# A new written order for the opening of a state-attention and feed-forward kernel, and a last tile scaled by one engine

## The chip, the cores and the metric

The kernel runs on one core of one Trainium2 chip. The metric is the time of one execution on the device in microseconds (us); the median of three runs is given. One of them, or one like them, was also taken with the hardware profiler, which records what each engine does and when. The engines are TensorE (PE in the rows, its weight loads PEld), VectorE (DVE), ScalarE (ACT), GpSimd (POOL) and SyncE (SP, which here only issues transfers).

## What is computed

Eight batches of eight heads attend between 512 tokens and 32 state rows of width 64, in both directions. The joined result (4352 rows of 512) goes through a feed-forward layer with a clipped activation.

```python
def _attn_ref(x, state):                      # x (8, 8, 512, 64), state (8, 8, 32, 64)
    scores = scale * np.matmul(x, state.transpose(0, 1, 3, 2))
    scores = scores - scores.max(-1, keepdims=True)
    a = np.exp(scores)
    a /= a.sum(-1, keepdims=True) + 1e-09
    xread = np.matmul(a, state)
    ...                                       # the same from state to tokens: sread
    return np.concatenate([xread, sread], axis=2)

def _moe_ref(x, w_in, w_out):                 # w_in (512, 2048), w_out (2048, 512)
    h = x @ w_in
    relu6 = np.clip(h + 3.0, 0.0, 6.0)
    g = h * relu6 / 6.0
    return g @ w_out
```

## The kernel before

**The work.** `xread @ w_in` is computed as the attention weights times `W = state @ w_in`, so a batch needs its weights `aT` and its `W` (tiles `wp`). A step n is one slice of 128 of the 2048 hidden columns of one batch: `first(n)` makes `ps_h` from `wp` and `aT`, ScalarE and VectorE make the activation `g`, and `second(n)`, two steps later, adds `g` times a slice of `w_out` into four accumulators `acc0` to `acc3`. A product in float32 is made of two halves of 32-bit operands (`hi`, `lo`) with three matmuls; `split` makes the halves with one pass on ScalarE and one on VectorE. The very first step and its `wp` stay whole float32 (L1011, L1059). There are 8 batches of 16 steps, and at the end 16 more steps for the state rows of all batches.

**The opening.** Before the first product of `first(0)` (L1011) batch 0 needs its attention weights. Its tokens come in four quarters of two heads each (tile `xb`, L496). Quarters 1 and 3 are issued by ScalarE's queue, behind the state (L452). Quarters 0 and 2 are issued by SyncE's queue, and the first slice of `w_in` (tile `early`, L387) stands between them. For each quarter q, TensorE turns the tokens into bank `acc{q}` (four transposes, L641), ScalarE copies them to `w_in3` (L645), and TensorE makes the scores (L708). The state is turned by one transpose (L610), and VectorE spreads it over `sread_t` with four copies (L619); the scores need these. Then the softmax of a quarter runs: VectorE takes the maximum (L719) and subtracts it (L727), ScalarE takes the exponential (L730), VectorE sums (L733). For two quarters at a time VectorE makes the reciprocal (L738), and the multiplication (L741) is GpSimd's for quarters 0 and 1 and VectorE's for quarters 2 and 3. TensorE turns the result (L750), the copies go to `w_in2` (L752, L753), and `first(0)` begins.

**The weights.** They come as loads of 64-bit words of which ScalarE writes the upper part (`tops`, L396) and VectorE joins both (L401). `W` for the first slices (L529) needs the joined `w_in0`.

**What sets the order.** Every operation is told to a `Plan` with an engine, a cost and a rank. The plan walks through them with its own clock and puts them in a row; each engine then runs its own in that order, and waits where data is missing. For the first operations the row isn't planned but written out: `OPENING` is a list of operation numbers. In it 0, 2, 3 and 4 are the loads of quarters 0, 1, 2 and 3, 1 is the state's load, 24 the first `w_in` load, 27 the state's transpose, 34, 36, 38 and 40 the transposes of the quarters, 42, 47, 54 and 59 their scores. Where the plan's clock sees TensorE idle before `first(0)`, `issue` puts small matmuls on constants there (L1442). 27 of them run.

**The end.** The last tile of the output is `acc1` times 1/6. It is cut in two: ScalarE scales columns 0 to 255, VectorE the others (L1087), and one transfer stores it.

Of the kernel before, what the change touches and what calls it, by code (L numbers as in the profile page):

```python
# [45 lines left out]


OPENING = """
# [25 lines left out]
"""  # L74


class Plan:
# [3 lines left out]


    AFTER = {"T": 0.25, "V": 0.12, "S": 0.12, "P": 0.15, "Q": 0.0}
    WARM = 5.9

    first_loads = 5

# [131 lines left out]
def tile_state_attention_then_hardswish_ffn(  # L219
# [8 lines left out]
    nc = tc.nc  # L228
    B, H, S, D = x.shape
    NS = state.shape[2]  # L230
    DFF = w_in.shape[1]
    DO = w_out.shape[1]
# [8 lines left out]
    NF = DFF // P  # L241
# [51 lines left out]
    def T(cost, rank, do, reads=(), writes=(), after=()):  # L293
        return plan.add("T", cost, rank, do, reads, writes, after)

    def V(cost, rank, do, reads=(), writes=(), after=()):
        return plan.add("V", cost * 1.08 if states_told else cost, rank, do, reads, writes, after)
# [307 lines left out]
    def take_in(b, rank, after=(), banks=None):  # L605

        st = ("ps_s", ("st", b))
        rank = rank if isinstance(rank, list) else [rank] * 3
        if b < TURNED:
            T(0.12, rank[0], lambda: nc.tensor.transpose(  # L610
                bank(st)[:, :P], made["st_raw", b], ident),
                [("st_raw", b)], [st], after)

        for r in range(2) if b < TURNED else ():
            for i in range(2):
                def put(r=r, i=i):
                    src = bank(st)[r * D : (r + 1) * D, :P].rearrange("p (q u m) -> p q u m", q=NQ, u=NG)
                    dst = apart[i * D : (i + 1) * D, :, :, i].rearrange("p q u (m r) -> p q u m r", r=2)
                    nc.vector.tensor_copy(dst[..., r], src)  # L619
                V(0.22, RANKS["apart"] if b == 0 else URGENT, put, [st], [("apart", b, r, i)])  # L620
        for u in range(NG) if b < TURNED else ():
            def together(u=u):
                rows = slice(u * D, (u + 1) * D)
                stT = get(("stT", b), lambda: att.tile([P, P], F32, name="stT"))
                nc.gpsimd.tensor_copy(
                    stT[rows].rearrange("p (q n) -> p q n", n=NS), apart[rows, :, u, u])
            kept.append(P_(0.3, RANKS["apart"], together, apart_parts(b), [("stT", b)]))
        for q in range(NQ):
            if b >= TURNED:
                key = ("raw", ("x", b, q // 2))  # L630
                V(0.7, rank[0], lambda q=q, key=key: nc.vector.transpose(  # L631
                    xT(b, q), made[key][:, q % 2]),
                    [(*key, q % 2, u, k) for u in range(2) for k in range(D // NS)], [xT_key(b, q)], after)
                continue
            ps = (banks[q] if banks else "ps_s", ("T", b, q))

            def turn(q=q, ps=ps):
                for u in range(NG):
                    for k in range(J // 2):
                        twos = x_tile(b)[:, NG * q + u, 2 * k : 2 * k + 2, :]  # L640
                        nc.tensor.transpose(  # L641
                            bank(ps)[:, (u * 2 + k) * P : (u * 2 + k + 1) * P],
                            twos.rearrange("p j d -> p (j d)"), ident)
            T(0.45, rank[1], turn, [(*x_key(b), "q", q)], [ps], after)
            S_(0.6, rank[2], lambda q=q, ps=ps: nc.scalar.copy(xT(b, q), bank(ps)), [ps], [xT_key(b, q)], [table])  # L645
# [42 lines left out]
    def tokens_by_rows(after, banks):  # L688
# [11 lines left out]
        for q in range(NQ):  # L700
# [3 lines left out]
            def scores(q=q, ps=ps):  # L704
                out = bank(ps)[:, : A * NS].rearrange("p (k i u n) -> p k u i n", k=J // 2, i=2, n=NS)
                for u in range(NG):
                    for k in range(J // 2):
# [6 lines left out]
            m1 = lambda m1_key=m1_key: get(  # L714
                m1_key, lambda: small.tile([P, S // NS], F32, name="m1"))[:, :A]
            r = RANKS["soft0"]
            scores_at[0] = T(0.93, RANKS["scores0"], scores,
                             apart_parts(0) + [xT_key(0, q)], [ps], after)
            V(0.34, r[0], lambda m1=m1, view=view: nc.vector.tensor_reduce(  # L719
                m1(), view(), axis=AX.X, op=ALU.max), [ps], [m1_key])  # L720
# [328 lines left out]
    def second(n):  # L1049
# [26 lines left out]
        for j in range(nt):  # L1076
            acc = (f"acc{j}", seg)
            rank = n + LAG
            if more:
                V(0.68, rank, lambda j=j, acc=acc: nc.vector.scalar_tensor_tensor(  # L1080
                    ot()[:, j, :], bank(acc), 1.0 / 6.0, ot()[:, j, :], op0=ALU.mult, op1=ALU.add),
                    [acc], [(*ot_key, j)])
            elif b == B and j == nt - 1:
                for add, engine, cs in (
                    (S_, nc.scalar.mul, slice(0, DO // 2)), (V, nc.vector.tensor_scalar_mul, slice(DO // 2, DO))
                ):
                    add(0.42, rank, lambda j=j, acc=acc, engine=engine, cs=cs: engine(  # L1087
                        ot()[:, j, cs], bank(acc)[:, cs], 1.0 / 6.0), [acc], [(*ot_key, j, cs.start)])
            elif b < B and (j % 2 == 0 or i < NF - 1):
                S_(0.62, rank, lambda j=j, acc=acc: nc.scalar.mul(ot()[:, j, :], bank(acc), 1.0 / 6.0),  # L1090
                   [acc], [(*ot_key, j)])
            else:
                V(0.68, rank, lambda j=j, acc=acc: nc.vector.tensor_scalar_mul(
                    ot()[:, j, :], bank(acc), 1.0 / 6.0), [acc], [(*ot_key, j)])
# [8 lines left out]
        else:  # L1103

            ov = out.rearrange("(b s) e -> s b e", s=TOK)
            for j in range(nt):
                rows = slice(S + j * P // B, S + (j + 1) * P // B)
                parts = [(*ot_key, j)] if j < nt - 1 else [(*ot_key, j, k * DO // 2) for k in range(2)]
                Q(n, 262.0, lambda j=j, rows=rows: nc.sync.dma_start(ov[rows], ot()[:, j, :]), parts)

    def half_of(t, k, s):
        return t[:, NG * k : NG * (k + 1), s * P : (s + 1) * P]
# [360 lines left out]
```

## Time and profile before

| | |
|---|---|
| three runs | 642.13, 642.19, 643.22 us, median 642.19 |
| span of the profiled execution | 640.3 us |
| median of the runs less that span | 1.89 us |
| TensorE busy | 632.0 us (99%) |
| VectorE busy | 428.8 us (67%) |
| ScalarE busy | 299.0 us (47%) |
| GpSimd busy | 2.9 us |
| TensorE's share in the chain that ended last | 97% |

The span runs from the first instruction's start to the end of the last transfer; the profiled execution's own time is given by its span alone. Busy time of TensorE counts a matmul from its start to a modelled end, so matmuls overlap in the rows: what one costs is the distance from start to start. A row's time counts from the start of the span.

### The profile page before, as it was taken

What the parts mean: (1) busy time and instruction counts of PE and PEld (TensorE: products, weight loads), DVE (VectorE), ACT (ScalarE), POOL (GpSimd) and SP (SyncE); (2) the same over time, 40 slices, a digit from 0 to 9 for tenths busy, and PEclk for the clock granted to TensorE, in tenths of its full rate; (3) what the DMA queues carried; (4) which work ended last, traced back from release to release, by engine and by line L of the source; (5) the groups of instructions that cost most, each with busy time, mean ns of one, the idle gap of its engine ahead of it and who ended that gap; (6) DMA issues with size and microseconds to landing.
All of it is one profiled execution on the core that took longest, in us unless ns stands there. A gap on an engine that the chain in (4) does not pass through costs nothing.

```text
span 640.3 us, 9853 instructions
## 1 busy us (share of the span) xinstructions
PE 632.0 (99%) x3810; PEld 492.2 (77%) x3810; DVE 428.8 (67%) x712; ACT 299.0 (47%) x509; POOL 2.9 (0%) x11
## 2 busy tenths in 40 slices
PE   7999999999999999999999999999999999999997
PEld 6677777877778787787778787787778778788885
DVE  6989994578595366945798566956699555454732
ACT  5997663434343343534454354534445353433331
POOL 1000000000000000000000000000000000000000
PEclk9999999999999999999999999999999999999999
DMA  8989203444331405144242626154332349076141
GB/s 274 380 235 243 76 2 63 91 124 86 97 67 22 78 1 137 66 117 115 105 131 55 185 64 163 65 120 113 132 68 76 90 148 346 33 245 215 67 131 34
DMA packets 143759, 77.71 MB, mean 121 GB/s; under 512 B 124512, under 2 KB 132320, under 8 KB 141792
## 3 DMA queue, kind: packets, MB, share of 16 engines
q1 hardware_dynamic: 143024, 76.49, 42.0%
q8 instruction: 30, 0.49, 0.3%
q10 hardware_dynamic: 688, 0.59, 0.3%
q14 instruction: 17, 0.14, 0.1%
HBM read 47.70 MB, written 23.59 MB: 111 GB/s over the span
## 4 chain that ended last, share of the span: by engine, by line
PE 97%; DMA 1%; DVE 1%; ACTq 0%; issue 0%; ACT 0%
PE acc L988 58%; PE ps_h L988 27%; PE ps_s L529 4%; PE ps_s L988 3%; PE ps_h L529 2%; PE ps_h L945 1%; DMA xb<-in_x_dram 1%; PE acc L1059 1%; PE ps_h L1011 0%; DVE w_in L401 0%; PE acc L641 0%; PE acc L750 0%; PE ps_s L945 0%; DVE s L733 0%; PE ps_s L883 0%; PE acc L708 0%
## 5 line engine op out<-in xcount | busy, mean ns | idle before, releaser
L988 PE MATMUL acc<-w_out_hi,g_hi 128*128 128x512 f32 x540 | 213.1, 395 | 0.0
L988 PE MATMUL acc<-w_out_lo,g_hi 128*128 128x512 f32 x540 | 210.3, 389 | 0.0
L988 PE MATMUL acc<-w_out_hi,g_lo 128*128 128x512 f32 x540 | 210.2, 389 | 0.0
L1040 ACT ACTIVATE g<-ps_h,three 128x512 f32<-128x512 f32 x128 | 88.0, 689 | 187.8 <-PE ps_h L988 184.8
L1042 DVE SCALAR_TENSOR_TENSOR g<-g,ps_h 128x512 f32<-128x512 f32 x128 | 87.6, 685 | 95.5 <-ACT g L1040 94.8
L988 PEld LDWEIGHTS acc<-w_out_hi,g_hi 128*128 128x128 f32 x540 | 101.3, 188 | 34.9 <-issue 13.0
L988 PEld LDWEIGHTS acc<-w_out_hi,g_lo 128*128 128x128 f32 x540 | 101.4, 188 | 21.3
L988 PEld LDWEIGHTS acc<-w_out_lo,g_hi 128*128 128x128 f32 x540 | 101.4, 188 | 20.2
L321 DVE TENSOR_TENSOR g_lo<-g,g_hi 128x512 fp32r<-128x512 f32 x127 | 86.9, 686 | 39.5 <-ACT g_hi L320 38.0
L320 ACT CAST g_hi<-g 128x512 fp32r<-128x512 f32 x127 | 78.7, 621 | 70.7 <-DVE g L1042 52.2
L988 PE MATMUL ps_h<-aT_hi,wp_hi 128*128 128x512 f32 x182 | 71.7, 394 | 0.0
L988 PE MATMUL ps_h<-aT_hi,wp_lo 128*128 128x512 f32 x182 | 70.8, 389 | 0.0
L988 PE MATMUL ps_h<-aT_lo,wp_hi 128*128 128x512 f32 x182 | 70.8, 389 | 0.0
L988 PE MATMUL ps_h<-aT_hi,wp 128*128 128x512 f32 x144 | 50.2, 389 | 0.0
L988 PEld LDWEIGHTS ps_h<-aT_hi,wp_hi 128*128 128x128 f32 x182 | 34.2, 188 | 8.1 <-issue 0.7
L988 PEld LDWEIGHTS ps_h<-aT_lo,wp_hi 128*128 128x128 f32 x182 | 34.2, 188 | 7.2 <-issue 0.3
L988 PEld LDWEIGHTS ps_h<-aT_hi,wp_lo 128*128 128x128 f32 x182 | 34.2, 188 | 7.1
L988 PEld LDWEIGHTS ps_h<-aT_hi,wp 128*128 128x128 f32 x144 | 27.0, 188 | 5.6
L988 PE MATMUL ps_h<-aT_lo,wp 128*128 128x512 f32 x72 | 28.0, 389 | 0.0
L321 DVE TENSOR_TENSOR wp_lo<-ps_h,wp_hi 128x512 fp32r<-128x512 f32 x18 | 11.8, 687 | 13.3 <-ACT wp_hi L320 13.3
L529 PE MATMUL ps_s<-w_in,stT 64*32 64x512 f32 (+1 forms) x304 | 19.0, 556 | 0.0
L631 DVE STREAM_TRANSPOSE tmp<-raw 128x512 f32<-128x512 f32 x28 | 18.9, 694 | 0.0
(161 smaller groups left out, 553.1 us busy)
## 6 DMA issues: line engine op xcount, KB each, us to landing
terms<-far SPq DMA_DIRECT2D x14, 1024.0 KB, 5.2
out_dram<-ot SPq DMA_DIRECT2D x8, 1024.0 KB, 4.4
xb<-in_x_dram SPq DMA_DIRECT2D x30, 256.0 KB, 4.2
raw<-in_x_dram SPq DMA_DIRECT2D x112, 64.0 KB, 2.5
far<-half SPq DMA_DIRECT2D x14, 512.0 KB, 2.9
far<-raw SPq DMA_DIRECT2D x14, 512.0 KB, 2.9
early<-in_moe_w_in_dram SPq DMA_DIRECT2D x5, 1023.0 KB, 6.4
raw<-raw SPq DMA_DIRECT2D x112, 32.0 KB, 2.0
```

Source lines behind the costliest of these rows:

```text
L320: S_(cost, rank, lambda: nc.scalar.copy(hi(), src()), reads, [writes[0]])
L321: V(cost, rank, lambda: nc.vector.tensor_tensor(lo(), src(), hi().bitcast(F32), op=ALU.subtract), [*reads, writes[0]], [writes[1]])
L529: nc.tensor.matmul(out[u][cols, :], made["stT", b][rows, cols], moving(q)[rows], start=True, stop=True,)
L631: V(0.7, rank[0], lambda q=q, key=key: nc.vector.transpose(xT(b, q), made[key][:, q % 2]), [(*key, q % 2, u, k) for u in range(2) for k in ...
L945: nc.tensor.matmul(bank(pr)[cols, u * D : (u + 1) * D], e2T(b, u)[:, j * P + q * NS : j * P + (q + 1) * NS], x_tile(b)[:, NG * q + u, j, : ...
L988: nc.tensor.matmul(ps, l, r, start=start and k == 0, stop=stop and k == n - 1)
L1040: S_(cost + 0.05, rank, lambda: nc.scalar.activation(g(), bank(ps)[:, :width], AF.Relu, bias=three), [ps], [g_key])
L1042: V(cost, rank, lambda: nc.vector.scalar_tensor_tensor(g(), g(), 6.0, bank(ps)[:, :width], op0=ALU.min, op1=ALU.mult), [ps], [g_key])
L1059: nc.tensor.matmul(bank(acc), made["g_hi", n][:, js], plain_out[i][1](), start=opens, stop=closes)
```

## The change

The written list is longer (it reaches to operation 989 instead of ending near 760) and in another order, three numbers of the plan's own clock differ (WARM, and the costs of the state's four copies and of the scores), and the last tile is scaled by ScalarE alone.

```diff
 OPENING = """
-1 0 34 2 27 4 29 31 5 30 24 28 36 35 42 37 43 40 3 25 44 26 41 32 45 33 47 48 38 49 59 46 73 60 39 54 70 50 74
...
+1 0 27 31 2 4 28 34 36 40 5 35 29 30 37 24 3 41 25 42 47 43 38 44 59 48 73 45 32 33 26 39 49 46 50 60 51 61 52
...
-    WARM = 5.9
+    WARM = 4.6
...
-                V(0.22, RANKS["apart"] if b == 0 else URGENT, put, [st], [("apart", b, r, i)])
+                V(0.3, RANKS["apart"] if b == 0 else URGENT, put, [st], [("apart", b, r, i)])
...
-            scores_at[0] = T(0.93, RANKS["scores0"], scores,
+            scores_at[0] = T(0.86, RANKS["scores0"], scores,
...
-            elif b == B and j == nt - 1:
-                for add, engine, cs in (
-                    (S_, nc.scalar.mul, slice(0, DO // 2)), (V, nc.vector.tensor_scalar_mul, slice(DO // 2, DO))
-                ):
-                    add(0.42, rank, lambda j=j, acc=acc, engine=engine, cs=cs: engine(
-                        ot()[:, j, cs], bank(acc)[:, cs], 1.0 / 6.0), [acc], [(*ot_key, j, cs.start)])
-            elif b < B and (j % 2 == 0 or i < NF - 1):
+            elif (j % 2 == 0 or i < NF - 1) if b < B else j == nt - 1:
                 S_(0.62, rank, lambda j=j, acc=acc: nc.scalar.mul(ot()[:, j, :], bank(acc), 1.0 / 6.0),
                    [acc], [(*ot_key, j)])
...
-                parts = [(*ot_key, j)] if j < nt - 1 else [(*ot_key, j, k * DO // 2) for k in range(2)]
-                Q(n, 262.0, lambda j=j, rows=rows: nc.sync.dma_start(ov[rows], ot()[:, j, :]), parts)
+                Q(n, 262.0, lambda j=j, rows=rows: nc.sync.dma_start(ov[rows], ot()[:, j, :]), [(*ot_key, j)])
```

TensorE, from the turning of the state or of the first quarter to the last scores, before. `acc0` to `acc3` in a row with `xb` are the four quarters being turned; rows with `sread_t` are scores, of quarter 0 and 1 in `ps_s`, of 3 in `acc1`, of 2 in `acc0`.

```order
L641 MATMUL acc1_134<-ident_84,xb_102 128x128 x4
L1442 LDWEIGHTS const-bfloat16-1.0
L1442 MATMUL ps_h_97<-const-bfloat16-1.0 128x256
L1442 LDWEIGHTS const-bfloat16-1.0
L1442 MATMUL ps_h_97<-const-bfloat16-1.0 128x256
L708 MATMUL ps_s_143<-sread_t_93,w_in3_139 128x2x32 x4
L641 MATMUL acc3_151<-ident_84,xb_102 128x128 x4
L708 MATMUL ps_s_166<-sread_t_93,w_in3_139 128x2x32 x4
L641 MATMUL acc2_173<-ident_84,xb_102 128x128 x4
L708 MATMUL acc1_179<-sread_t_93,w_in3_139 128x2x32 x4
L708 MATMUL acc0_190<-sread_t_93,w_in3_139 128x2x32 x4
```

The same place after the change. Line numbers are 11 higher there, from L85 to the code of the last tile. The state's transpose stands seven rows ahead of these, three of the small matmuls between.

```order
L652 MATMUL acc0_123<-ident_84,xb_102 128x128 x4
L652 MATMUL acc1_128<-ident_84,xb_102 128x128 x4
L652 MATMUL acc3_133<-ident_84,xb_102 128x128 x4
L719 MATMUL ps_s_149<-sread_t_93,w_in3_139 128x2x32 x4
L719 MATMUL ps_s_154<-sread_t_93,w_in3_139 128x2x32 x4
L652 MATMUL acc2_161<-ident_84,xb_102 128x128 x4
L719 MATMUL acc1_167<-sread_t_93,w_in3_139 128x2x32 x4
L719 MATMUL acc0_195<-sread_t_93,w_in3_139 128x2x32 x4
```

What moved: quarter 3 is turned before any scores, where it stood behind quarter 0's; quarter 0's scores come after it. Each engine runs as many instructions of each kind as before, but for the last tile.

VectorE, before, from the sum of quarter 0 to the multiplication of quarters 2 and 3 (`m1` maximum, `s1` sum and reciprocal, `ot` the exponentials, `tops` a join of weights).

```order
L733 TENSOR_REDUCE s1_184<-ot_95 128x8
L719 TENSOR_REDUCE m1_187<-acc1_179 128x8
L733 TENSOR_REDUCE s1_184<-ot_95 128x8
L727 TENSOR_TENSOR ot_95<-acc1_179,m1_187 128x8x32
L719 TENSOR_REDUCE m1_209<-acc0_190 128x8
L738 RECIPROCAL s1_184<-s1_184 128x8x2
L727 TENSOR_TENSOR ot_95<-acc0_190,m1_209 128x8x32
L401 SCALAR_TENSOR_TENSOR w_in0_159<-early0_131,tops_91 128x4x128
L733 TENSOR_REDUCE s1_184<-ot_95 128x8 x2
L738 RECIPROCAL s1_184<-s1_184 128x8x2
L741 TENSOR_TENSOR w_in2_253<-ot_95,s1_184 128x8x64
```

The same stretch after.

```order
L730 TENSOR_REDUCE m1_186<-acc1_167 128x8
L744 TENSOR_REDUCE s1_183<-ot_95 128x8
L738 TENSOR_TENSOR ot_95<-acc1_167,m1_186 128x8x32
L749 RECIPROCAL s1_183<-s1_183 128x8x2
L730 TENSOR_REDUCE m1_200<-acc0_195 128x8
L738 TENSOR_TENSOR ot_95<-acc0_195,m1_200 128x8x32
L744 TENSOR_REDUCE s1_183<-ot_95 128x8
L412 SCALAR_TENSOR_TENSOR w_in0_179<-early0_144,tops_91 128x4x128
L744 TENSOR_REDUCE s1_183<-ot_95 128x8
L749 RECIPROCAL s1_183<-s1_183 128x8x2
L752 TENSOR_TENSOR w_in2_193<-ot_95,s1_183 128x8x64
```

What moved: the first reciprocal (L738, now L749), which lets GpSimd multiply, stands ahead of the last maximum instead of behind it, and three passes over one quarter follow it where the join of the second slice of `w_in` (L401, now L412) followed after one. Ahead of these rows the join of the first slice now comes after quarter 1's maximum.

SyncE's queue, before, from its first transfer.

```order
L496 DMA xb_102<-in_x_dram 128x2x256
L387 DMA early0_131<-in_moe_w_in_dram 128x4x511
L496 DMA xb_102<-in_x_dram 128x2x256
L387 DMA early0_131<-in_moe_w_in_dram 128x4x511
L387 DMA early1_232<-in_moe_w_in_dram 128x4x1023
L387 DMA raw_237<-in_moe_w_out_dram 128x2047
L387 DMA raw_285<-in_moe_w_out_dram 128x2047
L387 DMA early0_300<-in_moe_w_in_dram 128x4x1023
```

And after.

```order
L507 DMA xb_102<-in_x_dram 128x2x256
L398 DMA early0_144<-in_moe_w_in_dram 128x4x511
L507 DMA xb_102<-in_x_dram 128x2x256
L398 DMA early0_144<-in_moe_w_in_dram 128x4x511
L398 DMA early1_234<-in_moe_w_in_dram 128x4x1023
L398 DMA raw_237<-in_moe_w_out_dram 128x2047
L398 DMA raw_239<-in_moe_w_out_dram 128x2047
L398 DMA raw_247<-in_moe_w_out_dram 128x2047
L398 DMA early3_315<-in_moe_w_out_dram 128x2047
L398 DMA early0_345<-in_moe_w_in_dram 128x4x1023
```

What moved: the first five transfers are the same in the same order (and so are ScalarE's three, the state and quarters 1 and 3); two more slices of `w_out` go ahead of the large `w_in` load that was eighth.

## Rows read from the trace of the kernel before

**Rows 1.** Busy time in one stretch: window, length, then us busy by engine

```profile
core 0: us, PE busy (x) PEld busy (x) DVE busy (x) ACT busy (x) POOL busy (x), PEclk, DMA share, GB/s
17.19:635.62 618.43, 618.41 (x3663) 481.46 (x3662) 417.18 (x685) 289.21 (x489) 0.00 (x0) 1.00 0.42 117
```

**Rows 2.** The chain that ended last, its opening: start, length, what

```profile
1.67 6.16 DMA xb<-in_x_dram
...
15.04 0.71 DVE w_in L741
```

**Rows 3.** The end of the timeline, and ScalarE's scaling of whole tiles (busy, mean ns)

```profile
635.64 0.42 DVE L1087 TENSOR_SCALAR ot<-acc 128x256 f32<-128x256 f32 x1 [0.67 <-PE acc L988]
636.10 0.38 ACT L1087 ACTIVATE ot<-acc 128x256 f32<-128x256 f32 x1 [4.36 <-DVE ot L1087]
...
L1090 ACT ACTIVATE ot<-acc 128x512 f32<-128x512 f32 x16 | 9.6, 597 | 2.7 <-PE acc L988 2.6
```

**Rows 4.** First loads: issue in the timeline; then loads by window, KB, us to landing

```profile
1.19 0.97 ACTq L496 DMA_DIRECT2D xb<-in_x_dram  x2
1.24 0.46 SPq L387 DMA_DIRECT2D early<-in_moe_w_in_dram  x1
...
1.74 0.52 SPq L496 DMA_DIRECT2D xb<-in_x_dram  x1
...
xb<-in_x_dram ACTq DMA_DIRECT2D x1, 256.0 KB, 3.5
...
early<-in_moe_w_in_dram SPq DMA_DIRECT2D x1, 511.0 KB, 5.6
xb<-in_x_dram ACTq DMA_DIRECT2D x1, 256.0 KB, 6.2
xb<-in_x_dram SPq DMA_DIRECT2D x1, 256.0 KB, 6.5
```

**Rows 5.** Timeline of TensorE: start, length, what, count, [idle before, and what ended it]

```profile
0.77 3.15 PE L1442 MATMUL ps_h<-const-bfloat16-1.0 128*128 128x256 bf16 x14 [0.77 <-PEq L1457]
...
3.83 0.96 PE L641 MATMUL acc<-ident,xb 128*128 128x128 f32 x4
...
4.74 0.66 PE L641 MATMUL acc<-ident,xb 128*128 128x128 f32 x4
...
6.36 1.08 PE L708 MATMUL ps_s<-sread_t,w_in 128*128 128x64 f32 x8 [0.74 <-DVE sread_t L619]
...
7.88 0.66 PE L641 MATMUL acc<-ident,xb 128*128 128x128 f32 x4 [0.44 <-DMA xb<-in_x_dram]
...
8.37 1.00 PE L708 MATMUL ps_s<-sread_t,w_in 128*128 128x64 f32 x8
...
9.65 1.94 PE L708 MATMUL acc<-sread_t,w_in 128*128 128x64 f32 x16
...
14.20 0.45 PE L529 MATMUL acc<-w_in,stT 64*32 64x128 f32 x16 [1.36 <-DVE w_in L401]
```

**Rows 6.** Timeline of VectorE and GpSimd in the opening

```profile
9.41 0.42 DVE L719 TENSOR_REDUCE m<-ps_s 128x8 f32<-128x256 f32 x1 [0.46 <-PE ps_s L708]
...
9.87 0.43 DVE L727 TENSOR_TENSOR ot<-ps_s,m 128x256 f32<-128x256 f32 x1
...
12.03 0.24 DVE L738 RECIPROCAL s<-s 128x16 f32<-128x16 f32 x1
...
12.45 1.05 POOL L741 TENSOR_TENSOR w_in<-ot,s 128x512 f32<-128x512 f32 x1 [5.46 <-ACT tmp L587]
12.48 1.56 DVE L401 SCALAR_TENSOR_TENSOR w_in<-early,tops 128x512 uint32<-128x512 uint32 x1
...
13.97 0.75 DVE L733 TENSOR_REDUCE s<-ot 128x8 f32<-128x264 f32 x2
```

**Rows 7.** Joins of another load, by shape: count, busy, mean ns

```profile
L401 DVE SCALAR_TENSOR_TENSOR raw<-raw,tops 128x512 uint32<-128x512 uint32 x7 | 4.8, 684 | 0.1
```

59 rows, old and new, of the table OPENING are left out of this document.

## The prediction

> **What bounds the kernel now.** I read the stretches first, then the chain, then the timelines of the two ends. From the first product of `first(0)` at 17.19 us to the end of the last at 635.62, TensorE is busy 618.41 of 618.43 us [rows 1]: in that stretch the reader is to see that nothing holds it up. An order can't shorten it, since every matmul stays; it can only make it longer. So the time is decided before 17.19 and after 635.62. Of the opening the chain says what ended last [rows 2]: the load of a quarter of the tokens, issued at 1.67, lands at 7.83; softmax work follows, up to VectorE's multiplication at 15.04, on which the products of `first(0)` wait. At the other end the two halves of the last tile don't run side by side: VectorE scales from 635.64 to 636.06, and ScalarE begins at 636.10 and ends at 636.48 [rows 3].
>
> **The change part by part: the last tile.** Whole tiles of this size take ScalarE 0.597 us [rows 3]. Begun at 635.64 it ends at 636.24, where the second half ended at 636.48: 0.24 less, on the path, since the last transfer waits for it. Had the halves run side by side, the edit would lose about 0.2; the rows say they don't.
>
> **The loads.** Their landings decide what may be moved ahead. Over both queues they land in the order of their issue [rows 4]: quarter 1 (issued at 1.19) 3.5 us later at 4.7, the first `w_in` slice (1.24) 5.6 later at 6.8, quarter 3 (1.67) 6.2 later at 7.8, quarter 2 (1.74) 6.5 later at 8.2. In the order rows SyncE's first five transfers and ScalarE's three are unchanged, and nothing ahead of them differs. So I leave all landings where they are; the first slice of weights still goes ahead of quarters 2 and 3. The two `w_out` slices that now go earlier stand in SyncE's queue behind all three `w_in` loads that the opening needs, and cost it nothing; that cover is gone only if transfers should overtake each other, which no row shows.
>
> **The state first; the plan's numbers.** The state's transpose and VectorE's four copies move ahead by about a microsecond. The first scores will wait for the tokens instead, so this is worth nothing; it would be due only if that wait went away. The three numbers are the plan's own clock and no instruction's cost; the small matmuls stay 27.
>
> **The new wait.** TensorE runs its queue in order. Before, quarter 0's scores ran at 6.36, while quarter 3 was on its way [rows 5], and VectorE made quarter 0's maximum and subtraction and the join of the first slice before 9.41. Now quarter 3's transposes stand ahead of all scores, and they wait for 7.83. Queued behind them are all four quarters' scores, and VectorE waits for those. TensorE idles from 5.40 (4.74 and 0.66) to 7.88, 2.48 us, where it idled 0.74 and 0.44 with work between. At 8.37, where quarter 1's scores stood, quarter 0's will begin; so VectorE takes quarter 0's maximum at 9.41, where it took quarter 1's [rows 5, 6].
>
> **VectorE from 9.41 to the multiplication.** Before, this was 5.63 us (9.41 to 15.04). I replay the new rows with these distances [rows 6]: after a pass over a quarter the next starts 0.34 later (two sums of 0.42 in 0.75); a pass that needs the one before starts 0.46 after it (9.41 to 9.87); a join, 0.68 long elsewhere [rows 7], lets the next start after 0.60, with the same 0.08 of overlap; the reciprocal after 0.16. Maximum 0 at 9.41, subtraction at 9.87; maximum 1 at 10.35 (its scores, eight records of 0.11 behind quarter 0's, end at 10.3); join at 10.69; subtraction at 11.29; sum 0 at 11.63; maximum 3 at 11.97; sum 1 at 12.31; subtraction at 12.65; reciprocal at 12.98; maximum 2 at 13.14; subtraction at 13.60; sum 3 at 13.93; join of the second slice at 14.27. TensorE doesn't bind: of its forty records from 7.88, 0.11 apart, quarter 3's scores end by 11.6 and quarter 2's by 12.5. ScalarE's exponentials each lie under a pass between.
>
> **GpSimd beside other passes.** Before, GpSimd multiplied from 12.45 to 13.50, and a join that VectorE began at 12.48 took 1.56 [rows 6] instead of 0.68: it ended 0.54 after GpSimd did, as if held until then, a loss of 0.88. Now the reciprocal at 12.98 lets GpSimd begin 0.42 later (as 12.03 to 12.45), from 13.40 to 14.45. Beside it VectorE has a maximum, a subtraction and a sum, and only then the join, which starts at 14.27 and, by the same 0.54, ends at 14.99, 0.04 late. The subtraction reads a bank and a small tile, the sum one tile; no row shows either beside GpSimd. If the subtraction were held like the join, from 13.60 to 14.45 and then 0.3 or so, the sums and the multiplication would come 0.85 later. I take the join alone, since the one held row is of its kind, and keep 0.85 for the upper side. The Trainium skill (SBUF — State Buffer, Who interferes with whom) says that a VectorE instruction with two inputs in SBUF contends with a GpSimd instruction that reads SBUF, and that one with at most one such input, outside some modes, doesn't. By that rule the join alone is held and the sum below stands; by the row read for any pass that touches SBUF it is 0.85 more.
>
> After the join the last sum starts at 14.92 and ends at 15.34; before, the multiplication began 0.32 after the sums' end (13.97 and 0.75, then 15.04) [rows 2, 6]. So it begins at 15.66 now, 0.62 later. In short: two passes and a join that were done ahead of 9.41 come after it (1.28), two short waits come with them (0.26), 0.84 of holding goes, and so does 0.08 of waiting that the old order had. Behind the multiplication the same chain follows, so `first(0)` begins 0.62 later. Bounds: 0.36 if the two waits are hidden, 1.47 with the held subtraction.
>
> **After `first(0)`.** The orders differ for some 90 us, but with the same passes on each engine, and the loads come no later than the opening does. The nearest row for a join that comes late for TensorE: 1.36 at 14.20 [rows 5]. Between nothing and 1.36 I take nothing, as TensorE waited for none in the old order [rows 1].
>
> **Sum.** Minus 0.24 and plus 0.62: 0.38 us more on a span of 640.3. What lies around the span, 1.89 us to the median, stays. 642.19 + 0.38 = **642.6 us**, which a measurement can't tell from no change: for this kernel that takes about 0.2%, 1.28 us.
>
> **Rivals.** *The clock falls.* The clock's column says 1.00 [rows 1], but the first small matmuls, 256 columns each, are 0.21 apart (14 in 3.15), which is 1.2 GHz, and four transposes take 0.96 at 3.83 and 0.66 at 4.74 [rows 5]: TensorE rose to 2.4 GHz near 4.5, after 3.7 us of work almost without a break. It stayed there through idle times of 0.74, 0.44 and 1.36 [rows 5]. 2.48 is nearly twice the longest of them. Should the clock fall there, the forty records from 7.88 go at half speed; if it takes the same 3.7 us to rise, half of that is lost, 1.85 us, and VectorE waits for it: 642.6 + 1.85 = 644.4. It decides if 2.48 us of idling is enough; no row here shows a fall. Chance 0.15. The Trainium skill (TensorE: Matmul & The Clock Gate, What's actually happening) says that TensorE goes back to 1.2 GHz when it has been idle, which speaks for this rival.
>
> *The tokens do land ahead of the weights.* If quarter 3 came right behind quarter 1, at the pace of the slice that does (511 KB from 4.69 to 6.84, so 1.08 for 256 KB) [rows 4], it would land at 5.77, 2.06 earlier. Everything of the replay from 7.83 on goes with it: the multiplication begins at 13.60, 1.44 before the old one, and with the end's 0.24 the time is 642.19 - 1.68 = 640.5. Against it: the unchanged issues, and landings that follow them [rows 4]. Chance 0.08.
>
> *GpSimd holds the subtraction too.* 642.6 + 0.85 = 643.4, about at the bound of 0.2%. Chance 0.09. *A late join behind `first(0)`.* 642.6 + 1.36 = 643.9. Chance 0.05. The forecast keeps 0.63.
>
> **How the numbers follow.** Faster by over 0.2% is the second rival alone, 0.08. Slower takes the clock (0.15), the late join (0.05) and half of the held subtraction (0.05): 0.25. The rest, 0.67, is no difference. The range reaches from 641.2, which is the forecast's lower bound, 642.3, less the 1.1 by which runs of one kernel differ here, to 644.3, which takes in the held subtraction, the late join and nearly half of the clock's case; the early tokens and the other half, 0.16, are left out.
>
> **What would show it.** Right: TensorE idle near 2.5 us before quarter 3's transposes, until the load; quarter 0's maximum at 9.4; the join's long row gone (about 0.7); the multiplication at 15.6 to 15.7 and `first(0)` near 17.8; one ScalarE pass of 0.6 at the end. Wrong: quarter 3 landing near 5.6; scores 0.21 apart after 8 us; a subtraction of over 1 us beside GpSimd; TensorE idle anywhere between `first(0)` and the end.

## The result, and the profile after

The changed kernel takes 647.12 us (median of 11 runs, 646.09 to 647.69); the kernel before, on the same chips, 643.22 (11 runs, 641.68 to 646.79). The ratio is 1.0055, 95% interval 1.0037 to 1.0073: 0.55% slower (the ratios here are estimated from the single runs, so they are not quite those of the medians), where 642.6 and no difference were forecast. Single runs of most kernels lie 2 to 5 us above the rest (24 of 111 of the kernel before are above 644.5), and all 11 runs of the changed one lie there. Of the 4.5 us between 642.6 and 647.12, 1.0 is in the kernel before itself, since the forecast started from 642.19.

The profiled execution has a span of 645.2 us, 4.9 more. First comes TensorE up to `first(0)`, to be read against [rows 5] (line numbers are 11 higher than before; a line of dots marks left-out rows):

```profile
0.77 2.29 PE L1446 MATMUL ps_h<-const-bfloat16-1.0 128*128 128x256 bf16 x10 [0.77 <-PEq L1461]
3.33 0.45 PE L621 MATMUL ps_s<-ident,st_raw 128*128 128x128 f32 x1 [0.27 <-DMA st_raw<-in_state_dram]
3.58 0.85 PE L1446 MATMUL ps_h<-const-bfloat16-1.0 128*128 128x256 bf16 x3
4.22 2.20 PE L652 MATMUL acc<-ident,xb 128*128 128x128 f32 x8
8.03 0.66 PE L652 MATMUL acc<-ident,xb 128*128 128x128 f32 x4 [1.61 <-DMA xb<-in_x_dram]
8.52 2.48 PE L719 MATMUL ps_s<-sread_t,w_in 128*128 128x64 f32 x16
10.80 1.06 PE L652 MATMUL acc<-ident,xb 128*128 128x128 f32 x4
11.65 3.52 PE L719 MATMUL acc<-sread_t,w_in 128*128 128x64 f32 x16
15.10 0.68 PE L540 MATMUL acc<-w_in,stT 64*32 64x128 f32 x16
15.52 1.96 PE L553 MATMUL ps_s<-w_in,sread_t 64*32 64x256 f32 x32
17.41 1.47 PE L1446 MATMUL ps_h<-const-bfloat16-1.0 128*128 128x256 bf16 x6
18.81 0.68 PE L540 MATMUL acc<-w_in,stT 64*32 64x128 f32 x16
...
20.19 1.03 PE L761 MATMUL acc<-ident,w_in 128*128 128x128 f32 x8
...
21.47 0.70 PE L1022 MATMUL ps_h<-w_in,tmp 128*128 128x512 f32 x1
```

The reader is to see two things. Quarter 3's transposes wait for their tokens, as forecast (8.03, after 1.61 idle). And the same four transposes that take 0.66 at 8.03 take 1.06 at 10.80; sixteen score records take 3.52 at 11.65. `first(0)` begins at 21.47 instead of 17.19, 4.28 later. The stretches of TensorE say why (length, busy time and instructions, granted clock, DMA share, GB/s):

```profile
6.00:8.00 2.00, 0.42 (x3) 1.00 1.06 345
8.00:10.00 2.00, 1.98 (x17) 0.91 1.06 389
10.00:14.00 4.00, 4.00 (x21) 0.50 1.05 409
14.00:18.00 4.00, 4.00 (x57) 0.50 0.58 226
18.00:20.00 2.00, 2.00 (x25) 0.53 0.73 192
20.00:24.00 4.00, 4.00 (x36) 1.00 1.09 407
```

The granted clock falls to half (1.2 GHz) at 9.65 us and stays there for 10.24 us, though TensorE is busy all that time. VectorE, to be read against [rows 6], waits for the slow scores, and its multiplication is at 17.68 instead of 15.04. GpSimd's multiplication (14.92 to 15.97) holds neither the maximum nor the subtraction that run beside it (0.42 each), and the long join is gone (0.68 at 16.34):

```profile
9.56 0.42 DVE L730 TENSOR_REDUCE m<-ps_s 128x8 f32<-128x256 f32 x1 [4.54 <-PE ps_s L719]
...
15.20 0.42 DVE L730 TENSOR_REDUCE m<-acc 128x8 f32<-128x256 f32 x1 [0.46 <-PE acc L719]
15.66 0.42 DVE L738 TENSOR_TENSOR ot<-acc,m 128x256 f32<-128x256 f32 x1
16.00 0.42 DVE L744 TENSOR_REDUCE s<-ot 128x8 f32<-128x264 f32 x1
16.34 0.68 DVE L412 SCALAR_TENSOR_TENSOR w_in<-early,tops 128x512 uint32<-128x512 uint32 x1
...
17.68 0.69 DVE L752 TENSOR_TENSOR w_in<-ot,s 128x512 f32<-128x512 f32 x1
```

GpSimd's row:

```profile
14.92 1.05 POOL L752 TENSOR_TENSOR w_in<-ot,s 128x512 f32<-128x512 f32 x1 [9.12 <-DVE s L749]
```

But `first(0)` doesn't wait for that multiplication any more. The chain that ended last (start, length, what; before in [rows 2]) runs through TensorE alone from 8.03 to `first(0)`:

```profile
8.03 0.66 PE acc L652 x4
...
17.48 1.40 PE ps_h L1446 x6
...
19.48 0.87 PE ps_h L1446 x5
20.35 0.87 PE acc L761 x8
21.23 0.33 PE ps_h L1446 x3
```

The transposes that turn the multiplication's result (L761) begin at 20.19, 1.82 after its end at 18.37. Fourteen small matmuls, which compute nothing, stand in the chain for 2.60 us.

Then the end, against [rows 3]:

```profile
640.25 0.39 PE L999 MATMUL acc<-w_out_hi,g_lo 128*128 128x512 f32 x1
640.68 0.60 ACT L1095 ACTIVATE ot<-acc 128x512 f32<-128x512 f32 x1 [3.90 <-PE acc L999]
```

One ScalarE pass begins 0.43 after the last matmul's start and ends at 641.28. From that matmul's start to the end of the span it is 4.93 us; before it was 5.10 (635.21 to the end). Between `first(0)` and the last matmul lie 618.79 us, before 618.02. Most of the difference is one wait:

```profile
588.68 0.70 PE L999 MATMUL ps_s<-terms,sums_hi 128*128 128x512 f32 x2 [0.42 <-DMA terms<-far]
```

It costs 0.58 (0.81 from the start of the matmul ahead instead of 0.23). Five of the nine profiles of the changed kernel and of those built on it have a wait ahead of `terms` (0.16 to 1.93 us), at different places; none of the five of the kernel before and of those built on that has one. Whether the change causes it isn't shown. The sum is 4.28 + 0.77 - 0.17 = 4.9.

### The profile page after: what moved, and what is told of

The parts are those of the page before. It is cut to its first block, busy times and chain, and to the rows that moved or that the text cites. A ratio compares the mean times of both kernels' runs of the same rounds, so it can differ in the third digit from the quotient of the medians.

```text
span 645.2 us, 9852 instructions
## 1 busy us (share of the span) xinstructions
PE 637.5 (99%) x3810; PEld 495.8 (77%) x3810; DVE 427.8 (66%) x711; ACT 299.4 (46%) x509; POOL 2.9 (0%) x11
## 4 chain that ended last, share of the span: by engine, by line
PE 95%; DMA 3%; SPq 1%; ACTq 0%; issue 0%; ACT 0%
PE acc L999 56%; PE ps_h L999 26%; PE ps_s L540 4%; PE ps_s L999 3%; PE ps_h L540 2%; DMA terms<-far 2%; PE ps_h L956 1%; DMA xb<-in_x_dram 1%; SPq L1231 1%; PE acc L1070 1%; PE acc L719 1%; PE ps_h L1446 0%; PE ps_s L719 0%; PE ps_h L1022 0%; PE acc L540 0%; PE ps_s L553 0%
```

## The experiments

In all of them the whole order is written out, and a table SMALL says how many small matmuls stand ahead of which operation; else each is the kernel it names. Times are medians, the kernel before beside them is from the same chips. "High" counts the runs above 644.5 us. A run's mean granted clock tells a fall too: 10.24 us at half of it make 0.992 (an estimate from the profile of the changed kernel), and 9 of that kernel's 11 runs have 0.989 to 0.992.

**The wait filled (e1).** The changed kernel, with

```diff
-SMALL = {27: 10, 34: 3, 81: 6, 66: 5, 101: 3}
+SMALL = {27: 10, 34: 3, 40: 7, 81: 6, 66: 5, 101: 3}
```

> The changed kernel with seven more small matmuls on TensorE ahead of quarter 3's transposes, where it idled 1.61 us. Theory 1 (that idling lets the granted clock fall from 2.4 to 1.2 GHz at 9.65): the clock stays at 2.4 GHz, first(0) begins near 18.0 instead of 21.47, and the time is 643.0 to 643.9. Theory 2 (the clock falls because the first run of small matmuls is broken by 0.27 us ahead of the state's transpose and the first rise so comes late): the clock falls as before, first(0) at 21 to 21.5, 646.5 to 647.3. Theory 3 (the clock costs little, the new order does): the clock stays up and first(0) still begins after 20, 646 or more.

643.14 against 642.59, ratio 0.9998 (0.9973 to 1.0023), 3 of 12 high. The profile:

```profile
6.43 1.52 PE L1446 MATMUL ps_h<-const-bfloat16-1.0 128*128 128x256 bf16 x7
7.99 0.66 PE L652 MATMUL acc<-ident,xb 128*128 128x128 f32 x4
8.49 1.90 PE L719 MATMUL ps_s<-sread_t,w_in 128*128 128x64 f32 x16
10.22 0.60 PE L652 MATMUL acc<-ident,xb 128*128 128x128 f32 x4
10.67 1.94 PE L719 MATMUL acc<-sread_t,w_in 128*128 128x64 f32 x16
...
15.72 0.69 DVE L752 TENSOR_TENSOR w_in<-ot,s 128x512 f32<-128x512 f32 x1
...
17.87 1.98 PE L1022 MATMUL ps_h<-w_in,tmp 128*128 128x512 f32 x4
```

With seven matmuls that compute nothing in the wait the clock stays at 2.4 GHz: the scores of quarters 3 and 2 take 1.94 instead of 3.52, and `first(0)` comes 3.60 us earlier. The multiplication is at 15.72 (forecast 15.66) and `first(0)` at 17.87 (forecast 17.8). None of the 12 runs has a mean granted clock under 0.997, so the three high ones don't show a fall of that length. Theory 1 holds, and theory 3 falls.

**Quarter 0's scores ahead of quarter 3's transposes (e2).** The changed kernel, with

```diff
-1 0 27 31 2 4 28 34 36 40 5 35 29 30 37 24 3 41 25 42 47
+1 0 27 31 2 4 28 34 36 5 35 29 30 37 24 3 42 40 41 25 47
```

> The changed kernel with quarter 0's scores ahead of quarter 3's transposes on TensorE, as in the kernel before; state first and small matmuls as changed. Theory 1 (the idling): it is cut in two by the scores, the clock stays at 2.4 GHz, first(0) at 17.2 to 17.8, 642.7 to 643.6. Theory 2 (the broken first run): the clock falls all the same, first(0) at 20 or later, 646 or more. Theory 3 (the order of the new wait itself): first(0) near 17.5 whatever the clock does.

642.45 against 642.59, ratio 1.0001 (0.9977 to 1.0026), 4 of 12 high. The profile keeps 2.4 GHz, TensorE idles 0.24 and 0.48 instead of 1.61, and `first(0)` is at 16.81, 0.39 ahead of theory 1's range; theory 2's fall is not there. Late in the profiled run TensorE waits 1.93 before 585.80, again ahead of `terms`.

**The wait alone (e3).** The kernel before, with

```diff
-28 36 35 42 37 43 40 3 25 44 26 41 32 45
+28 36 35 37 40 3 25 41 42 43 44 26 32 45
```

and its two small matmuls ahead of 40 instead of 42.

> The kernel before with one thing changed: quarter 3's transposes ahead of quarter 0's scores on TensorE (the new wait alone; the first run of fourteen small matmuls unbroken, two more before the wait). Theory 1: the clock falls as in the changed kernel, first(0) near 21, 646 to 647. Theory 2: no fall; the new wait alone costs what the replay gave, first(0) 17.6 to 18.3, 643.5 to 644.2. Theory 3: first(0) at 20 or later with the clock at 2.4 GHz.

643.52 against 642.59, ratio 1.0025 (0.9998 to 1.0053), 4 of 11 high (a twelfth run took 912.5 us and isn't counted). In the profile the clock stays at 2.4 GHz and `first(0)` is at 18.53, 1.34 later than before and 0.23 behind theory 2's range; the time is theory 2's. So this wait alone, in the old order, need not bring the fall: of the 11 runs one has a mean granted clock under 0.998 (0.989). Here quarter 1's tokens landed late (6.03), so that the idling was cut up: 0.57, two small matmuls, 1.02.

**The state first alone (e4).** The kernel before, with

```diff
-1 0 34 2 27 4 29 31 5 30 24 28 36
+1 0 27 31 28 29 30 2 4 34 5 24 36
```

and ten small matmuls ahead of 27, three ahead of 34.

> The kernel before with one thing changed: the state's transpose and its four copies first, with ten small matmuls ahead of it and three behind, as in the changed kernel (the break in the first run alone; quarter 0's scores stay ahead of quarter 3's transposes). Theory 1: the clock stays at 2.4 GHz once risen, first(0) at 17.0 to 17.4, the time that of the kernel before within 0.1%. Theory 2: the rise comes after 6 us and the clock falls again near 9.65, first(0) at 20 or later, 646 or more. Theory 3: as theory 1.

642.91 against 642.59, ratio 0.9988 (0.9964 to 1.0011), 1 of 12 high; `first(0)` at 17.04. The break in the first run, 0.55 here, costs nothing by itself: theory 2 (the broken run) fails, as in e2.

**The old order without small matmuls, first try (e5).** By a slip the table held its usual numbers: this is the kernel before again.

> The kernel before, its order untouched, without its 27 small matmuls, so that TensorE is idle until the first tokens land. Theory 1 (the price is that of TensorE at 1.2 GHz, in either order): the clock is still at 1.2 GHz for the scores at 6 to 12, the records there stand 0.21 apart, and first(0) begins at 20 to 22, 645.5 to 647.5. Theory 2 (the old order hides a slow TensorE, only the new one suffers): first(0) at 17.2 to 18.5, 642.2 to 643.7.

643.01 against 642.61, ratio 1.0015 (0.9995 to 1.0035), 4 of 11 high. It tells two things all the same. The same program's first recorded rise to 2.4 GHz stands at 6.67 us here and at 4.52 in the first profile. And its four high runs have mean granted clocks of 0.990 to 0.992, as most runs of the changed kernel: the old order seems to meet the fall now and then, too.

**Filled and unbroken (e6).** The changed kernel with `SMALL = {27: 14, 40: 7, 81: 6, 66: 5, 101: 3}`.

> The changed kernel with the seven small matmuls ahead of quarter 3's transposes, and with the first run unbroken (fourteen in one run, then the state's transpose). Theory 1 (idling decides the clock): the rise comes near 4.5 to 5, no fall, first(0) at 17.6 to 18.0, and no run of it, or one, above 644.5. Theory 2 (something else lifts single runs): runs above 644.5 as often as in the kernel before, about a quarter.

643.75 against 642.61, ratio 1.0014 (0.9994 to 1.0033), 2 of 11 high, `first(0)` at 17.81. It is no better than the filling alone: the break doesn't matter. Two high runs (at 0.996 and 0.999 of the clock) are one more than theory 1 allows and about as many as theory 2 says, so they decide nothing.

**Scores first, filled (e7).** The order of the second experiment with `SMALL = {27: 14, 42: 2, 40: 3, 81: 6, 66: 5, 101: 3}`.

> The changed kernel with quarter 0's scores ahead of quarter 3's transposes, an unbroken first run of fourteen small matmuls, two ahead of the scores and three ahead of quarter 3's transposes. First(0) at 16.7 to 16.9 as in the run without the fillings, time 641.7 to 642.2; by theory 1 hardly a run above 644.5, by theory 2 a quarter of them.

642.24 against 642.61, ratio 0.9996 (0.9978 to 1.0014), none of 11 high, `first(0)` at 16.94: theory 1, as far as 11 runs can tell.

**The tokens really ahead (e8).** The changed kernel, its order up to operation 84

```diff
+1 0 27 31 2 3 24 4 28 34 36 5 35 29 30 37 42 38 43 39 47 44 48 40 41 45 54 49 50 59 32 33 46 73 55 51 56 57
+25 52 53 60 61 62 74 26 58 70 71 72 63 64 65 75 86 6 14 126 66 68 67 87 11 81 84
```

and `SMALL = {27: 14, 42: 3, 38: 2, 66: 4, 101: 3}`.

> The changed kernel with the tokens really ahead of the weights: SyncE issues quarter 2 before the first slice of w_in; quarter 2 is worked on before quarter 3, the joins of the first two slices go behind the softmax passes, and the fillings are kept. If landings follow issues: quarter 2 at 5.5 to 6.0, quarter 3 at 6.8 to 7.2, the first slice near 8.5 to 9, VectorE's multiplication at 12.3 to 13, first(0) at 14.4 to 15.2, and 639.6 to 640.6 if nothing behind first(0) is late. Rival 1: quarter 3 lands at 7.8 as ever, first(0) past 16, 641.5 or more. Rival 2: the weights come too late, TensorE stands still behind first(0), 641 or more.

645.92 against 642.61, ratio 1.0055 (1.0042 to 1.0067), all 5 runs high. This is rival 1: quarter 2 landed at 5.40, but quarter 3, whose issue is unchanged, at 7.84 (7.83 before), as if it shared the way with the slice issued 0.07 us after it, which landed at 9.0. TensorE then idled 2.77 us for the first join (10.73 to 13.50), and the clock fell within that stretch:

```profile
10.00:12.00 2.00, 0.73 (x7) 1.00 1.02 379
12.00:14.00 2.00, 0.50 (x17) 0.53 1.02 414
14.00:18.00 4.00, 4.00 (x57) 0.50 0.94 331
```

**Unbroken, the wait not filled (e9).** The changed kernel with `SMALL = {27: 14, 81: 6, 66: 5, 101: 3}`.

> The changed kernel with nothing but the first run of small matmuls unbroken (fourteen, then the state's transpose); the wait for quarter 3 is not filled. Theory A (the unfilled wait alone is enough for the clock to fall in the new order): first(0) at 20.5 to 21.5 and nearly all runs at 646 to 647.5, as in the changed kernel. Theory B (break and wait are needed together): first(0) at 17.7 to 18.0, most runs at 642.8 to 643.5, a quarter of them higher, as in the run of the kernel before with the wait alone.

647.39 against 642.55, ratio 1.0063 (1.0045 to 1.0082), 11 of 11 high, eight of them at 0.989 to 0.992 of the clock. Theory A holds:

```profile
3.93 1.59 PE L652 MATMUL acc<-ident,xb 128*128 128x128 f32 x8
7.36 0.66 PE L652 MATMUL acc<-ident,xb 128*128 128x128 f32 x4 [1.83 <-DMA xb<-in_x_dram]
7.85 2.96 PE L719 MATMUL ps_s<-sread_t,w_in 128*128 128x64 f32 x16
...
20.84 2.00 PE L1022 MATMUL ps_h<-w_in,tmp 128*128 128x512 f32 x4
```

The clock falls at 8.46, again for 10.24 us.

**The tokens ahead, the clock looked after (e10).** The changed kernel, its order up to operation 11

```diff
+1 0 27 31 2 3 24 4 28 34 36 5 35 29 30 37 42 38 43 39 47 44 45 40 48 41 32 33 49 54 50 46 73 55 25 51 52 53
+59 56 57 60 61 62 58 26 74 126 70 71 72 63 64 65 75 86 87 66 68 67 69 89 88 81 84 85 82 83 90 6 14 11
```

and `SMALL = {27: 14, 42: 3, 70: 10, 66: 5, 101: 2}`.

> Quarter 2 loaded ahead of the first slice of w_in, as in the run before it, with the clock looked after: the late scores and ten small matmuls fill the stretch in which TensorE waited for the first join, and that join stands ahead of quarter 3's sum. If the idle stretch of 2.8 us was what let the clock fall there: no fall, VectorE's multiplication at 13.1 to 13.6, first(0) at 15.3 to 15.8, 640.0 to 641.2. Rival 1: the clock falls all the same, first(0) past 18, 644 or more. Rival 2: first(0) is early and TensorE then waits for weights, 641.5 to 643.

642.02 against 642.55, ratio 0.9974 (0.9953 to 0.9995), none of 11 high: faster than both kernels. But its median is only 0.5 us lower than that of the kernel before, of which 6 of 27 runs are high. No fall, the multiplication at 13.26, `first(0)` at 15.71, 1.48 earlier than before. But much is given back, as rival 2 has it:

```profile
19.21 0.69 DVE L412 SCALAR_TENSOR_TENSOR raw<-raw,tops 128x512 uint32<-128x512 uint32 x1
19.82 0.68 DVE L1053 SCALAR_TENSOR_TENSOR g<-g,ps_h 128x512 f32<-128x512 f32 x1
...
20.55 2.07 PE L1070 MATMUL acc<-raw,g 128*128 128x512 f32 x4 [0.37 <-DVE g L1053]
```

From `first(0)` to the first product of `second(0)` it takes 4.84 us (before 4.00, 17.19 to 21.19): VectorE's `g` stands behind a join of `w_out`. Another 0.83 is a wait ahead of `terms` at 597.90.

**The old order without small matmuls (e11).** The kernel before with `SMALL = {}`.

> The kernel before, its order untouched, now really without its 27 small matmuls (the run that was meant to be this one still had them and was the kernel before again). Theory 1 (the price is that of TensorE at 1.2 GHz, in either order): the scores at 6 to 12 stand at half speed, first(0) at 20 to 22, 645.5 to 647.5. Theory 2 (the old order hides a slow TensorE): first(0) at 17.2 to 18.5, 642.2 to 643.7.

646.9 against 642.55, ratio 1.0055 (1.0034 to 1.0075), 11 of 11 high. Theory 1 holds: at 1.2 GHz the old order loses as much as the new one, `first(0)` at 21.19:

```profile
8.82 1.06 PE L641 MATMUL acc<-ident,xb 128*128 128x128 f32 x4
9.68 1.81 PE L708 MATMUL ps_s<-sread_t,w_in 128*128 128x64 f32 x8
11.28 1.06 PE L641 MATMUL acc<-ident,xb 128*128 128x128 f32 x4
12.13 3.51 PE L708 MATMUL acc<-sread_t,w_in 128*128 128x64 f32 x16
```

The clock's column says 1.00 in this stretch, since no change was recorded before 18.35; the durations tell. The mean granted clock of these 11 runs is 0.997 to 0.999, so such a mean can hide a slow opening.

**Two in the wait (e12).** The changed kernel with `SMALL = {27: 14, 40: 2, 81: 6, 66: 5, 101: 3}`.

> The changed kernel with the unbroken first run and two small matmuls ahead of quarter 3's transposes, as many as stood there in the run of the kernel before with the wait alone; without them all 11 runs were above 645.8, with seven of them 9 of 11 were below 644.5. Theory A (how much of the wait is filled decides how often the clock falls): runs of both kinds, at 642.8 to 643.6 and above 645.5, some in each. Theory B (what else differs in the new order decides, two small matmuls change nothing): at least ten in eleven above 645.5.

648.63 against 642.25, ratio 1.0094 (1.0066 to 1.0123), 6 of 6 high, all at 0.989 to 0.992 of the clock: theory B, as far as six runs can tell. Two small matmuls are not enough here, where seven were. In the profile quarter 3 landed late, at 8.43; TensorE idled 2.46 all the same, and the clock fell at 8.39 for 13.65 us.

## Why the prediction was wrong

**The step that failed** is the rival of the clock: its mechanism was named, but it got a chance of 0.15 and a price of 1.85 us, and the forecast kept TensorE at 2.4 GHz. The chance was too low: three idle times without a fall, the longest 1.36 [rows 5], were read as a margin, though the new wait was worked out at nearly twice that, and no row spoke for a clock that holds through it. The small matmuls stayed 27, as forecast, but the forecast didn't ask where they stand: none stands in the new wait. With seven there, 3 of 12 and 2 of 11 runs are high and none has the mean clock of the fall (e1, e6); without them, 11 of 11 and 11 of 11 are high (the changed kernel, e9). So in the new order the unfilled wait is the cause, and e9 shows that it needs no broken first run. The Trainium skill (TensorE: Matmul & The Clock Gate, What's actually happening) says that TensorE returns to 1.2 GHz when it has been idle. The falls behind 1.61, 1.83 and 2.46 us and within 2.77 agree; an idle stretch of 1.70 us in e3 brought none.

The price was too low by half. It assumed a fall by 7.88, 3.7 us of work to bring the clock back, as at the start, and VectorE as the engine that waits. The clock fell at 9.65 and stayed down for 10.24 us, through 4.00 of 4.00 us busy, and 3.60 us of `first(0)` hang on it (21.47 against 17.87). Up to the multiplication it is 1.96 (17.68 against 15.72), near 1.85 by luck, since neither the fall nor the rise was where the price had them. The other 1.64 come behind it, where the price had nothing: TensorE's own queue, with fourteen small matmuls at 1.2 GHz in it, is the chain there, and not VectorE. How much the small matmuls alone cost isn't shown; no run leaves them out of the changed kernel.

**The tail.** The scaling ends 1.02 us after the last matmul's start instead of 1.27, so 0.25 earlier, as worked out (0.24). At the end of the span about 0.16 of it is left: from the last matmul's start to the end it takes 4.92 to 4.95 us in the nine profiles with this tail, 5.09 to 5.10 in the five with the old one. The step was right, its size 0.08 too large; where the rest went isn't shown.

**The loads.** Right: quarter 3 landed at 7.98, and the order of landings is the old one, so the second rival's case did not come about. With quarter 2 issued ahead of the slice (e8) quarter 2 came 2.8 us earlier and quarter 3 no earlier (7.84; 7.45 in e10), far from that rival's 5.77; a quarter 3 issued earlier was not tried.

**State first.** Right: it is worth nothing (e4).

**The new wait.** The place is right, and quarter 0's maximum stands at 9.56 (forecast 9.41). TensorE idled 1.61, not 2.48, because quarter 1's tokens landed at 5.31 instead of 4.69 and its transposes ran at 1.2 GHz.

**VectorE's replay and GpSimd.** Right, where the clock holds: 15.72 and 17.87 in e1 against 15.66 and 17.8. The wait alone, without GpSimd's new place, costs 1.34 (e3) where the replay's parts give 1.28 + 0.26 - 0.08 = 1.46. With GpSimd's new place, and VectorE's new order with it, the multiplication is 0.66 earlier (16.38 in e3, 15.72 in e1) where the replay gave back 0.84. The rival of the held subtraction falls: beside GpSimd it takes its usual 0.42. That agrees with the Trainium skill (SBUF — State Buffer, Who interferes with whom), by which a VectorE instruction with at most one input in SBUF, outside some modes, doesn't contend with GpSimd.

**After `first(0)`.** Right within half a microsecond: from `first(0)` to the last matmul's start it takes 618.48 in e1, 618.26 in e9 and, without its wait ahead of `terms`, 618.21 in the changed kernel, where it takes 618.02 to 618.28 in the old order. That wait, which the forecast did not have, is the only one of TensorE there.

**What stays open.** Why the new order falls with two small matmuls in the wait (e12) and the old order with nearly the same wait mostly doesn't (e3). The length of an idle stretch alone doesn't decide it: the 1.70 of e3, ending at 15.53, is longer than the 1.61 behind which the changed kernel fell. Nor is it shown what makes 24 of 111 runs of the kernel before high: of the 100 with a mean clock on record, 22 are high, and only 6 of these have 0.989 to 0.992, while 14 have 0.998 or more. A slow opening that the column doesn't show, as in e11, would fit them, but these runs have no profile.

## What to carry to other kernels

A wait that is moved on TensorE is priced twice: by what stands behind it, and by the clock. Where a change opens a new wait on TensorE, fill it with matmuls that compute nothing, and try how many it takes: seven were enough here, two were not. Price a fall over a measured length at half speed (6.83 to 13.65 us here), ask which engine is the chain then, and count the small matmuls that stand in its way. Read the clock from the durations of one shape as well as from its column, which shows nothing before the first recorded change.

## What was not expected of the hardware

The fallen clock did not rise in 10.24 us in which TensorE was busy throughout (in e12 it stayed down for 13.65, in e8 for 6.83, the first 1.37 of them idle). And the program alone doesn't set the first rise: it stands at 4.52 and 6.67 in two profiles of the kernel before. In the other kernels that begin with ten or fourteen small matmuls it stands between 3.92 (e7) and 7.63 (e1).
